# A planned instruction order made anew: a port shared by two engines, a cap on filling matmuls, other stage offsets

## The chip, the cores and the metric

The kernel runs on one core of a Trainium2 chip. The core has a matmul engine (TensorE, PE in the profile; its weight loads are listed apart as PEld), VectorE (DVE), ScalarE (ACT), GpSimd (POOL) and SyncE (SP), which issues transfers. Each engine works through its own queue in order; semaphores hold an instruction until what it needs is there. The metric is device time in microseconds (us), the median of several runs.

## What is computed

Three blocks follow each other, on 4 batches: a recurrence over 768 steps for 32 heads of width 40, a mixing block with a two-dimensional Fourier transform and an MLP, and a second mixing block with two MLPs (w_tok1 768x256, w_tok2 256x768, w_ch1 320x1536, w_ch2 1536x320; those of the first block 320x1280 and 1280x320). The weights arrive in double precision.

```python
for t in range(S):                                  # B=4, H=8, S=768, D=40
    y[:, :, t] = einsum('bhd,bhde->bhe', rt, state)
    Sa = einsum('bhde,bhe->bhd', state, at)
    state = state * wt[:, :, None, :] - einsum('bhd,bhe->bhde', Sa, bt) + einsum('bhd,bhe->bhde', vt, kt)
...
u = x + real(fft(fft(x, axis=1), axis=2))           # x: 4 x 768 x 320
un = (u - mean(u)) / sqrt(var(u) + 1e-06)
x = u + maximum(un @ w_ch1, 0) @ w_ch2
...
h = maximum(x.transpose(0, 2, 1) @ w_tok1, 0) @ w_tok2
u = x + h.transpose(0, 2, 1)
out = u + maximum(u @ w_ch1, 0) @ w_ch2
```

## The kernel before

**First stage, the recurrence (class `Attn`).** It is worked out in 12 chunks of 64 steps, all heads together (33 places in 11 groups of 3). For each chunk: the loads (wS, bt, a, LT, VZt, VZd, r); `decay`, the running products of w as two DVE scans (Q L262, R L265, with a reciprocal L264 between) and their products into a (L269) and bt (L274), on DVE for the first chunks and on POOL afterwards; `kg`, matmuls (L297) whose results are moved into RT (L303 and on ACT) and masked on POOL (L307). Parts of RT go through memory (Gd) into N. For each pair of chunks `inv` forms 32x32 triangular inverses on DVE alone: a copy to start (L333), then pairs of a product into pr (L331) and a sum (L332), copies L337 and L345, and last the copy into MT (L353). The tiles N, Mt, MT and pr exist once. The inverse leaves through memory (Ad, Md) and comes back as AT and Mst for the `merge` matmuls (mg L372, mc L382). `chain` is the step from chunk to chunk: x (L424) from the state LT, its copy bdX (L429), z (L436), s (L448), then on DVE the addition of s to LT in four pieces (L452), on POOL their product (L454), and so the next x. `outp` makes the chunk's result: matmuls st, zt, sc (L486) and y (L504, L508), masks on DVE (L491) and POOL (L496), and evictions into ys (L521, stored) or straight into X (L514) for the last chunks. So an inverse needs kg of its pair, kg needs RT free from an x five chunks earlier, and z of a pair needs its inverse.

**Beside it,** `wdec` (12 jobs) and `decode` (44 jobs) split the weights into a high and a low part: four DVE instructions each (L571 to L575; L780, L781, L783, L784), one on ACT and two on POOL.

**Then the MLPs (class `Mlp`).** `fft`: F, ef and the low part Xl on DVE (L805 to L815), psA matmuls (L824), evictions A on ACT and DVE (L831 to L833), a mirrored copy of A on ACT (L836); `fft2`: mix (L851); normalization, transposes (trp L888), the channel MLP (hps L917, acc L907, with hh on ACT and hl on DVE) and the two of the second block (tps, t2ps). 384 to 447 us is where one stage runs into the other.

**What sets the order.** All instructions are handed to `Plan` as operations with an engine, a cost in us and the tiles that they read and write. `emit` first works out a latest start for each (from a due time of the stage, costs and hand-over times `LATE`, `EXTRA` and `LATE_SAME`), adds an offset of its stage and chunk from the table `OFF`, and then plays the kernel through: at each step it takes the engine that can start first, and there, of the operations that are ready, the one with the earliest latest start. `HOLDBACK` lets an engine wait for one that is due much earlier. The order that comes out is the order in which each engine's queue is written; no time of the plan is kept in the program. Before an operation of TensorE that would have to wait, `fill` puts dummy matmuls `warm` on the identity (L52) into the planned gap: `FILL` holds the planned time of one and a count of columns. If the columns planned over the last `TICK` are under the count, the whole gap is filled.

## Time and profile before

| | |
|---|---|
| median of 3 runs | 1033.73 us (1024.39 to 1034.62) |
| profiled execution: span | 1027.9 us; its own time is not given apart from it |
| TensorE busy | 993.2 us, 97%; of it `warm` 101.5 us, 760 records |
| DVE busy | 635.6 us, 62% |
| ACT, POOL busy | 422.8 and 339.8 us |
| chain that ended last | TensorE 73%, DVE 14%, transfers 6% |
| first z, last y, first hps | 92.7, 406, 446.6 us |

One `warm` matmul is two records of the trace, so 760 records are 380 matmuls. The span is the time from the first to the last instruction of the profiled execution. The chain that ended last is followed back from the last instruction; a line of it says where the end came from, and the busy shares alone do not. The three marks divide the span: up to the first z the first inverse is made, up to the last y the chunks follow each other, and from the first hps on the MLPs run.

### The profile page before, as it was taken

To read this page: it belongs to the slowest core of one execution; us is meant where nothing else is said; L and a number is where in the kernel's file an instruction comes from. 1 tells how busy PE (TensorE), PEld (TensorE's weight loads), DVE (VectorE), ACT (ScalarE), POOL (GpSimd) and SP (SyncE) were. 2 spreads that over 40 slices of the span, in tenths; PEclk is the share of its full clock that TensorE was granted. 3 is DMA by queue.
4 is the path that set the end of the run, shared out by engine and by line. 5 is a ranking of instruction groups with operands and counts; after the bars stand their busy time and mean duration, and the time that the engine had idled before them with its cause. 6 is when DMAs were issued, how large, how long until landed. Compare 5 with 4: busy or idle time off the path is not lost.

```text
span 1027.9 us, 24475 instructions
## 1 busy us (share of the span) xinstructions
PE 993.2 (97%) x10135; PEld 951.4 (93%) x10135; DVE 635.6 (62%) x1346; ACT 422.8 (41%) x870; POOL 339.8 (33%) x425
## 2 busy tenths in 40 slices
PE   8898999899999999899999999999999999999998
PEld 8897888787888988899999999999999999999998
DVE  7598589788978539797888885334432432332322
ACT  4256587686766755342343422223221221221221
POOL 8584377668754544302344434100000000000000
PEclk9999699999999999899999999999999999999999
DMA  9986596989877887822454545900000000000000
GB/s 209 196 169 149 132 210 144 183 183 218 185 177 163 229 236 217 276 66 68 146 158 158 166 142 162 377 1 1 1 20 1 20 1 20 20 1 20 20 21 19
DMA packets 140722, 125.51 MB, mean 122 GB/s; under 512 B 100867, under 2 KB 118275, under 8 KB 140483
## 3 DMA queue, kind: packets, MB, share of 16 engines
q1 hardware_dynamic: 135811, 100.29, 39.6%
q0 software_dynamic: 4800, 23.67, 6.7%
q8 instruction: 79, 1.29, 0.6%
q14 instruction: 32, 0.26, 0.1%
HBM read 85.40 MB, written 33.75 MB: 116 GB/s over the span
## 4 chain that ended last, share of the span: by engine, by line
PE 73%; DVE 14%; DMA 6%; issue 2%; POOL 2%; SPq 2%; ACT 1%; DVEq 0%; POOLq 0%; ACTq 0%
PE hps L917 22%; PE acc L907 21%; DVE pr L331 4%; PE warm L52 4%; PE sc L486 3%; PE mix L851 3%; PE psA L824 2%; PE kg L297 2%; PE t2ps L994 2%; PE tps L981 2%; DMA Mst<-Md 2%; PE y L508 2%; SPq L217 1%; PE trp L888 1%; PE x L424 1%
## 5 line engine op out<-in xcount | busy, mean ns | idle before, releaser
L920 DVE SCALAR_TENSOR_TENSOR hl<-hps,hh 128x384 fp32r<-128x384 f32 x176 | 97.8, 556 | 239.0 <-ACT hh L919 238.4
L919 ACT ACTIVATE hh<-hps 128x384 fp32r<-128x384 f32 x176 | 86.4, 491 | 306.9 <-PE hps L917 306.9
L917 PE MATMUL hps<-th,v 128*128 128x384 f32 x576 | 143.0, 338 | 0.0
L907 PE MATMUL acc<-v,hh 128*128 128x320 f32 x576 | 129.5, 311 | 0.0
L917 PE MATMUL hps<-th,W 128*128 128x384 f32 x480 | 119.7, 339 | 0.9 <-DVE th L893 0.6
L907 PE MATMUL acc<-W,hh 128*128 128x320 f32 x480 | 107.9, 311 | 0.0
L52 PE MATMUL warm<-ident 128*128 128x128 f32 x760 | 101.5, 288 | 5.4 <-DVE A L833 3.4
L917 PEld LDWEIGHTS hps<-th,v 128*128 128x128 f32 x576 | 103.8, 188 | 0.2
L52 PEld LDWEIGHTS warm<-ident 128*128 128x128 f32 x760 | 96.2, 202 | 6.6 <-issue 3.5
L907 PEld LDWEIGHTS acc<-v,hh 128*128 128x128 f32 x576 | 97.6, 188 | 0.0
L785 POOL TENSOR_TENSOR mda<-mda,mdh 128x320 f32<-128x320 f32 (+2 forms) x44 | 44.4, 1009 | 153.9 <-ACT mdh L782 111.0
L917 PEld LDWEIGHTS hps<-th,W 128*128 128x128 f32 x480 | 86.8, 188 | 2.5 <-DVE th L893 1.0
L907 PE MATMUL acc<-v,hl 128*128 128x320 f32 x288 | 89.0, 309 | 0.0
L907 PEld LDWEIGHTS acc<-W,hh 128*128 128x128 f32 x480 | 80.8, 188 | 0.0
L907 PE MATMUL acc<-W,hl 128*128 128x320 f32 x240 | 74.0, 308 | 0.0
L917 PE MATMUL hps<-tl,v 128*128 128x384 f32 x192 | 64.6, 337 | 0.0
L307 POOL TENSOR_SCALAR_AFFINE_SELECT RT<-RT 64x384 f32<-64x384 f32 x72 | 52.6, 756 | 33.7 <-ACT RT L219 32.3
L297 PE MATMUL kg<-am,bt 120*128 120x192 f32 x242 | 52.2, 352 | 8.0 <-issue 2.6
L486 PE MATMUL sc<-rm,VZd 120*128 120x192 f32 x264 | 57.0, 350 | 2.1 <-DMA VZd<-in_vR_dram 1.0
L907 PEld LDWEIGHTS acc<-v,hl 128*128 128x128 f32 x288 | 54.1, 188 | 0.0
L917 PE MATMUL hps<-tl,W 128*128 128x384 f32 x160 | 53.9, 337 | 0.0
L496 POOL TENSOR_SCALAR_AFFINE_SELECT sc<-sc 64x384 f32<-64x384 f32 (+1 forms) x72 | 44.0, 612 | 27.3 <-ACT sc L219 24.7
(175 smaller groups left out, 2090.7 us busy)
## 6 DMA issues: line engine op xcount, KB each, us to landing
bt<-in_bkR_dram SPq DMA_DIRECT2D x12, 660.0 KB
mdraw<-in_moe_w_ch_dram SPq DMA_DIRECT2D x22, 320.0 KB
wS<-in_wR_dram SPq DMA_DIRECT2D x12, 335.2 KB
a<-in_aR_dram SPq DMA_DIRECT2D x12, 335.2 KB
RT<-a SPq DMA_DIRECT2D x36, 111.7 KB
LT<-in_vT_dram SPq DMA_DIRECT2D x12, 330.0 KB
VZt<-in_vT_dram SPq DMA_DIRECT2D x12, 330.0 KB
r<-in_rR_dram SPq DMA_DIRECT2D x12, 330.0 KB
```

The source lines that it names most:

```text
L52: for x in range(m): nc.tensor.matmul(t[:,128*(x%4):128*(x%4)+128],lhsT=ident,rhs=ident,start=True,stop=True)
L297: nc.tensor.matmul(ps[:,192*x:192*x+192],lhsT=bt[:,g+x].rearrange("p v t -> p (v t)"),rhs=am[:,:,g+x],start=True,stop=True)
L307: nc.gpsimd.affine_select(out=kv,in_=kv,pattern=[[0,3*m],[1,L]],compare_op=ALU.is_gt,fill=0.0,base=0,channel_multiplier=-1)
L331: P.op('DVE',.16+.0012*st[0]*shape[0],lambda: V.tensor_tensor(out=pr,in0=a,in1=b,op=ALU.mult),rd,[('pr',h)])
L486: for x,g in enumerate(gs): nc.tensor.matmul(ps[:,192*x:192*x+192],lhsT=VZd[:,g].rearrange("p v t -> p (v t)"),rhs=s.rm[:,:,g],start=True, ...
L496: nc.gpsimd.affine_select(out=o,in_=o,pattern=[[0,3*m],[1,L]],compare_op=ALU.is_gt,fill=0.0,base=0,channel_multiplier=-1)
L785: P.op('POOL',.06+d*.0028,lambda: nc.gpsimd.tensor_tensor(out=g("da").bitcast(F32),in0=g("da").bitcast(F32),in1=g("dh").bitcast(F32),op=AL ...
L851: nc.tensor.matmul(s.pst(h)[:,:320],lhsT=aa[:K,sl],rhs=T2[:K,tb],start=n==0,stop=n==7)
L907: nc.tensor.matmul(s.pst(acc[x]),lhsT=a[:,sl],rhs=t[w2][w][:,m],start=(m==0 and n==0),stop=(m==MT-1 and n==2))
L917: for n,(l,r) in enumerate(ops): nc.tensor.matmul(ps,lhsT=l,rhs=r,start=n==0,stop=n==7)
L919: s.act(384,lambda: nc.scalar.activation(out=t["hh"][z],in_=s.pst(h),func=AF.Relu),[kp],[('hh',z)],free=[h[0]])
L920: s.dve(.47,lambda: nc.vector.scalar_tensor_tensor(out=t["hl"][z],in0=s.pst(h),scalar=0.0,in1=t["hh"][z].bitcast(F32),op0=ALU.max,op1=ALU. ...
```

## The change

The planner gets one more rule, other costs and other offsets, and so a new order of the same instructions.

- An operation has a flag `port`: set for POOL operations without a transfer (not for memsets) and for those DVE operations that read two inputs from the on-chip memory, and some copies. `held` keeps which engine holds the port pair and until when. An operation with the flag starts, in the plan, only when the other engine has let go; among those that are ready the time it would wait counts with the weight `PW` against it.
- The costs are new: hand-over times smaller, scans 1.56 for 1.84, POOL's masks and products cheaper, issuing a transfer .5 for .64 (SP) and for 1.1 (POOL), DVE's decode .24 for .38 and alike. TensorE's costs are as before.
- `fill` puts in at most as many `warm` as bring the count of columns up to `FILL[1]`, which is 8203.8 for 9558.7; that is 17 at most in one gap.
- `HOLDBACK` is 1110 for 394.6, and every number of `OFF` is new.

```diff
-LATE={'ACT':.16,'DVE':.18,'POOL':.1,'PE':.3}
-EXTRA={'ACT':.08,'DVE':.035}
-LATE_SAME={'DVE':.03,'ACT':.03}
+LATE={'ACT':.135,'DVE':.115,'POOL':.09,'PE':.25}
+EXTRA={'ACT':.01}
+LATE_SAME={}
...
+        o.port=(eng=='POOL' and not data) if port is None else port
...
-        dma=0.0
+        dma=0.0; held=[None,0.0]
+        def port(o): return held[1] if o.port and held[0]!=o.eng else 0.0
...
-            m=0; o=Op(); o.eng='PE'; o.idx=-1; o.deps=[]; o.cost=FILL[0]; o.cols=512.0; a=t+.1
-            while b and a+FILL[0]<=end: a=s.pe(a,o); m+=1
+            m=0; top=-int(-(FILL[1]-w)//512); o=Op(); o.eng='PE'; o.idx=-1; o.deps=[]; o.cost=FILL[0]; o.cols=512.0; a=t+.1
+            while b and m<top and a+FILL[0]<=end: a=s.pe(a,o); m+=1
...
-                if pick is None or lst[o.idx]<lst[pick.idx]: pick=o
+                l=lst[o.idx]+PW*max(port(o)-t,0.0)
+                if pick is None or l<best: pick,best=o,l
...
-            engines[e]=s.pe(t,o) if e=='PE' else t+o.cost
+            b=max(t,port(o))
+            engines[e]=s.pe(b,o) if e=='PE' else b+o.cost
+            if o.port: held=[e,engines[e]]
...
-HOLDBACK=394.60
+PW=54.4
+HOLDBACK=1110.0
...
-OFF={'chain': -53.3, 'dec2': -42.2, 'decay': -47.7, 'decode': -65.8, 'fft': 52.7, 'fft2': -1.1, 'inv': 6.1,
+OFF={'chain': -50.3, 'dec2': 73.3, 'decay': -47.8, 'decode': -137.2, 'fft': 137.1, 'fft2': -148.5, 'inv': 6.5,
...
-FILL=(0.22,9558.7)
+FILL=(0.22,8203.8)
```

Each engine has the same instructions after as before, save for `warm`: 254 matmuls for 380, of which 114 for 226 stand ahead of the first z, 103 for 79 from there to the last z, 3 for 25 from there to the first psA, and 24 for 40 from there to the first hps. Lines are 4 to 5 higher in the changed kernel (L331 is L335, L805 is L810).

The first place is DVE's queue in the middle and at the end of the first inverse. Q, R and wS are the operands of the scans, D those of the reciprocal, pr, MT and Mt the inverse's. Before, the middle:

```order
L331 TENSOR_TENSOR pr_121<-Mt_119,MT_120 128x512 x2
L332 TENSOR_REDUCE Mt_119<-pr_121 128x8x8 x2
L262 SCALAR_TENSOR_TENSOR Q_112<-wS_111,D_113 120x715
L345 COPY MT_120<-Mt_119 128x256
L264 RECIPROCAL D_114<-Q_112 120x11
L331 TENSOR_TENSOR pr_121<-N_118,MT_120 128x256
L331 TENSOR_TENSOR pr_121<-N_118,MT_120 128x512
L332 TENSOR_REDUCE MT_120<-pr_121 128x16x4
L265 SCALAR_TENSOR_TENSOR R_126<-wS_111,D_114 120x715
L332 TENSOR_REDUCE MT_120<-pr_121 128x16x4
```

After, its end and the start of the second inverse (the last row):

```order
L336 TENSOR_REDUCE Mt_119<-pr_121 128x2x16
L269 SCALAR_TENSOR_TENSOR R_130<-wS_110,D_114 120x715
L336 TENSOR_REDUCE Mt_119<-pr_121 128x2x16
L357 COPY MT_120<-Mt_119 128x1024
L266 SCALAR_TENSOR_TENSOR Q_112<-wS_111,D_113 120x715
L268 RECIPROCAL D_114<-Q_112 120x11
L269 SCALAR_TENSOR_TENSOR R_126<-wS_111,D_114 120x715
L337 COPY Mt_119<-N_118 128x4
```

The scans Q and R of chunk 5 (R_126) stood in the middle and stand behind the copy of MT; R of chunk 4 (R_130) has moved from the inverse's start to its end, and a third scan Q that stood further on in it is gone from it.

The second place is DVE's queue in the third inverse, with the additions to the state (LT_136). Before, where they begin:

```order
L331 TENSOR_TENSOR pr_121<-Mt_119,MT_120 128x512 x2
L332 TENSOR_REDUCE Mt_119<-pr_121 128x8x8 x2
L452 TENSOR_TENSOR LT_136<-s,LT_135 40x320
L345 COPY MT_120<-Mt_119 128x256
L452 TENSOR_TENSOR LT_136<-s,LT_135 40x320
L331 TENSOR_TENSOR pr_121<-N_118,MT_120 128x256
L331 TENSOR_TENSOR pr_121<-N_118,MT_120 128x512
L332 TENSOR_REDUCE MT_120<-pr_121 128x16x4
L452 TENSOR_TENSOR LT_136<-s,LT_135 40x320
L265 SCALAR_TENSOR_TENSOR R_128<-wS_111,D_114 120x715
L332 TENSOR_REDUCE MT_120<-pr_121 128x16x4
```

After, where the same inverse ends:

```order
L335 TENSOR_TENSOR pr_121<-Mt_119,MT_120 128x448
L336 TENSOR_REDUCE Mt_119<-pr_121 128x2x16 x2
L357 COPY MT_120<-Mt_119 128x1024
L456 TENSOR_TENSOR LT_136<-s,LT_135 40x320 x4
L266 SCALAR_TENSOR_TENSOR Q_112<-wS_110,D_113 120x715
L268 RECIPROCAL D_114<-Q_112 120x11
L433 COPY bdX_142<-x 64x8x40
```

The four additions stood between the pairs of the inverse and stand behind its last copy, ahead of bdX.

The third place is TensorE's queue ahead of the first mix (psA and Xh are of `fft`, A of its evictions). Before:

```order
L824 MATMUL psA_5621<-T_4838,Xh 128x192 x2
L824 MATMUL psA_5621<-T_4838,Xl 128x192
L824 MATMUL psA_5637<-T_4838,Xh 128x192 x2
L824 MATMUL psA_5637<-T_4838,Xl 128x192
L52 MATMUL warm<-ident 128x128 x23
L851 MATMUL mix<-T_5481,A_5482 128x320 x2
L851 MATMUL mix<-T_5481,A_5483 128x320
```

After:

```order
L829 MATMUL psA_5430<-T_4739,Xl 128x192
L829 MATMUL psA_5441<-T_4739,Xh 128x192 x2
L829 MATMUL psA_5441<-T_4739,Xl 128x192
L52 MATMUL warm<-ident 128x128 x17
L856 MATMUL mix<-T_5452,A_5453 128x320 x2
L856 MATMUL mix<-T_5452,A_5454 128x320
```

Both have a filling there, of 23 matmuls before and of 17 now.

The last is DVE's queue at the evictions A that this filling and mix wait for; mdt and mda belong to the decoding of weights. Before:

```order
L806 TENSOR_TENSOR ef_4847<-F 128x3x159
L833 TENSOR_TENSOR A_5486<-psA_5545,A_5486 64x193
L781 SCALAR_TENSOR_TENSOR mda_5489<-mdraw_5487,mdt_5488 128x320
L832 TENSOR_TENSOR A_5485<-psA_5621,A_5484 128x193
L783 TENSOR_SCALAR mdt_5488<-mda_5489 128x320
L832 TENSOR_TENSOR A_5483<-psA_5637,A_5482 128x193
L780 TENSOR_SCALAR mdt_4850<-mdraw_4849 128x320
L784 SCALAR_TENSOR_TENSOR mdt_5488<-mdraw_5487,mdt_5488 128x320
L833 TENSOR_TENSOR A_5486<-psA_5545,A_5486 64x192
L832 TENSOR_TENSOR A_5485<-psA_5621,A_5484 128x192
L832 TENSOR_TENSOR A_5483<-psA_5637,A_5482 128x192
```

After:

```order
L810 TENSOR_TENSOR F<-X 128x960
L811 TENSOR_TENSOR ef_4934<-F 128x3x159
L838 TENSOR_TENSOR A_5457<-psA_5406,A_5457 64x193
L837 TENSOR_TENSOR A_5456<-psA_5430,A_5455 128x193
L837 TENSOR_TENSOR A_5454<-psA_5441,A_5453 128x193
L817 TENSOR_TENSOR Xl<-ef_4933,Xh 128x3x33
L838 TENSOR_TENSOR A_5457<-psA_5406,A_5457 64x192
L837 TENSOR_TENSOR A_5456<-psA_5430,A_5455 128x192
L837 TENSOR_TENSOR A_5454<-psA_5441,A_5453 128x192
```

The decode instructions stood between the evictions of A and are gone from there; from the first F up to the evictions one decode job of four instructions is left of about six.

## Rows read from the trace of the kernel before

**Rows 1.** The page, part 2: TensorE's granted clock in 40 slices of the span.

```profile
PEclk9999699999999999899999999999999999999999
```

**Rows 2.** Windows, all engines: stretch, length, busy us (count), PEclk, DMA share, GB/s.

```profile
0.00:93.00 93.00, 84.26 (x853) 82.13 (x854) 70.17 (x106) 44.66 (x70) 65.41 (x82) 0.98 0.86 183
...
120.00:384.00 264.00, 250.96 (x4732) 220.57 (x4732) 202.81 (x381) 186.72 (x357) 166.55 (x216) 0.99 0.83 190
...
447.00:1028.00 581.00, 575.95 (x3714) 572.58 (x3712) 287.49 (x673) 150.57 (x337) 76.50 (x86) 1.00 0.21 68
```

**Rows 3.** Windows for the tile warm alone, same columns, TensorE only.

```profile
0.00:93.00 93.00, 56.57 (x452) 55.24 (x452) 0.98 0.86 183
93.00:384.00 291.00, 23.61 (x158) 20.74 (x158) 0.96 0.81 186
384.00:447.00 63.00, 18.47 (x130) 17.45 (x130) 0.92 0.75 232
447.00:1028.00 581.00, 2.87 (x20) 2.76 (x20) 1.00 0.21 68
```

**Rows 4.** Timeline of DVE, start: start us, us, instruction, [idle before, released by].

```profile
21.41 0.88 DVE L278 TENSOR_SCALAR rm<-a,hm 120x704 f32<-120x704 f32 x1
...
25.94 1.65 DVE L262 TENSOR_TENSOR_SCAN Q<-wS,D 120x715 f32<-120x715 f32 x1 [1.04 <-POOL R L268]
...
40.27 1.65 DVE L262 TENSOR_TENSOR_SCAN Q<-wS,D 120x715 f32<-120x715 f32 x1 [10.36 <-DMA wS<-in_wR_dram]
```

**Rows 5.** Timeline of DVE, first inverse and start of the second.

```profile
41.83 0.14 DVE L333 COPY Mt<-N 128x4 f32<-128x4 f32 x1
...
46.42 1.94 DVE L331 TENSOR_TENSOR pr<-Mt,N 128x196 f32<-128x196 f32 x1
...
56.34 1.80 DVE L262 TENSOR_TENSOR_SCAN Q<-wS,D 120x715 f32<-120x715 f32 x1
...
60.57 2.30 DVE L265 TENSOR_TENSOR_SCAN R<-wS,D 120x715 f32<-120x715 f32 x1
...
68.27 1.93 DVE L262 TENSOR_TENSOR_SCAN Q<-wS,D 120x715 f32<-120x715 f32 x1
...
77.01 1.30 DVE L353 COPY MT<-Mt 128x1024 f32<-128x1024 f32 x1
...
83.44 0.57 DVE L333 COPY Mt<-N 128x4 f32<-128x4 f32 x1 [3.48 <-DMA Ad<-MT]
```

**Rows 6.** Timeline of POOL beside it.

```profile
46.30 1.70 POOL L269 TENSOR_TENSOR a<-a,R 120x715 f32<-120x715 f32 x1 [9.90 <-DMA a<-in_aR_dram]
```

**Rows 7.** Windows of line L331 (pr) over the inverses: length, busy (count).

```profile
41.80:78.40 36.60, 16.90 (x22) 0.95 0.87 180
83.40:117.60 34.20, 12.20 (x22) 0.78 0.58 126
...
sum 237.40, DVE 84.99; mean DVE 14.17
```

**Rows 8.** Timeline, third inverse: last LT addition and bdX on DVE; TensorE's x.

```profile
158.59 0.49 DVE L452 TENSOR_TENSOR LT<-s,LT 40x320 f32<-40x320 f32 x1
...
171.76 0.90 DVE L429 COPY bdX<-x 64x320 f32<-64x320 f32 x2
...
164.31 1.13 PE L424 MATMUL x<-LT,RT 128*64 128x40 f32 x32
```

**Rows 9.** Chain that ended last, 380 to 430 us: start us, us, what.

```profile
395.32 0.32 DVE mdt L780
...
418.99 0.40 DVE mdt L784
```

**Rows 10.** Timelines of ACT and TensorE before the first mix.

```profile
419.81 1.35 ACT L836 ACTIVATE A<-A 128x384 fp32r<-128x384 f32 x3 [0.52 <-DVE A L833]
...
419.93 7.00 PE L52 MATMUL warm<-ident 128*128 128x128 f32 x46 [3.39 <-DVE A L833]
```

**Rows 11.** Windows around the stretch at the lower clock, columns as in rows 2.

```profile
102.80:120.00 17.20, 17.20 (x192) 14.56 (x194) 12.09 (x25) 6.31 (x12) 4.63 (x8) 0.50 0.53 144
```

More of the change, by code (lines that the diff above doesn't have):

```diff
@@ L54 @@
 class Op:
-    __slots__=('eng','cost','fn','deps','succ','due','alloc','free','data','idx','fin','nwait','ready','rel','cols','stage','pools')
-LATE={'ACT':.16,'DVE':.18,'POOL':.1,'PE':.3}
-EXTRA={'ACT':.08,'DVE':.035}
-LATE_SAME={'DVE':.03,'ACT':.03}
+    __slots__=('eng','cost','fn','deps','succ','due','alloc','free','data','idx','fin','nwait','ready','rel','cols','stage','pools','port')
+LATE={'ACT':.135,'DVE':.115,'POOL':.09,'PE':.25}
+EXTRA={'ACT':.01}
+LATE_SAME={}
 class Plan:
@@ L64, in __init__, with op @@
         s.ops=[]; s.w={}; s.r={}; s.banks=banks; s.stage=None; s.filler=None
-    def op(s,eng,cost,fn,R=(),W=(),due=None,alloc=None,free=(),data=0.0,rel=0.0,after=(),cols=0.0,pools=None):
-        o=Op(); o.cols=cols; o.stage=s.stage; o.pools=pools; o.rel=rel; o.eng,o.cost,o.fn,o.due,o.data=eng,cost+EXTRA.get(eng,0.0),fn,due,data
+    def op(s,eng,cost,fn,R=(),W=(),due=None,alloc=None,free=(),data=0.0,rel=0.0,after=(),cols=0.0,pools=None,port=None):
+        o=Op(); o.cols=cols; o.stage=s.stage; o.pools=pools; o.port=(eng=='POOL' and not data) if port is None else port; o.rel=rel; o.eng,o.cost,o.fn,o.due,o.data=eng,cost+EXTRA.get(eng,0.0),fn,due,data
         o.alloc=[] if alloc is None else alloc if isinstance(alloc,list) else [alloc]
@@ L220, in zero @@
     def zero(s,t,W,cost=.3):
-        s.P.op('POOL',cost,lambda: s.nc.gpsimd.memset(t,0.0),(),W)
+        s.P.op('POOL',cost,lambda: s.nc.gpsimd.memset(t,0.0),(),W,port=False)
     def one(s,t,W,v=1.0):
-        s.P.op('POOL',.1,lambda: s.nc.gpsimd.memset(t,v),(),W)
+        s.P.op('POOL',.1,lambda: s.nc.gpsimd.memset(t,v),(),W,port=False)
     def init(s):
@@ L344, in inv @@
         d0=16*33; K=((0,4),(4,4),(8,2),(10,2),(12,2),(14,2))
[L345 removed]
+        P.op('DVE',.29,lambda: V.tensor_copy(out=tt(512,[16,16],[1,16]),in_=mm(d0,[1,16],[32,16])),['m8',('m16',1)],['mt2'],port=True)
         for t0,w in K:
@@ L352, in inv @@
         mk=['m8','Mt']+[('m16',m) for m in range(2)]+[('m32',x) for x,_ in K]
-        P.op('DVE',1.08,lambda: V.tensor_copy(out=s.MT,in_=s.Mt.rearrange("p i j -> p j i")),mk,['MT','mt1','mt2']+[('t2',x) for x,_ in K])
+        P.op('DVE',.97,lambda: V.tensor_copy(out=s.MT,in_=s.Mt.rearrange("p i j -> p j i")),mk,['MT','mt1','mt2']+[('t2',x) for x,_ in K],port=True)
         for x in range(2):
@@ L544, in out_tile @@
         P.op('NONE',0.0,close,[],keys+['close'])
-        for k in range(3): P.op('POOL',1.0,lambda k=k: nc.gpsimd.dma_start(out=s.T1[:,k],in_=s.T1d[128*k:128*k+128]),['close'],[('T1',k)],data=2.2)
+        for k in range(3): P.op('POOL',.5,lambda k=k: nc.gpsimd.dma_start(out=s.T1[:,k],in_=s.T1d[128*k:128*k+128]),['close'],[('T1',k)],data=2.2)
         for x in range(f):
@@ L693, in pe, with dve @@
         s.P.op('PE',cost,fn,R,W,alloc=alloc,due=s.now,cols=cols); s.now+=cost
-    def dve(s,cost,fn,R,W,free=()): s.P.op('DVE',cost,fn,R,W,free=free)
+    def dve(s,cost,fn,R,W,free=(),port=False): s.P.op('DVE',cost,fn,R,W,free=free,port=port)
     def act(s,n,fn,R,W,free=()): s.P.op('ACT',.05+n/1200,fn,R,W,free=free)
@@ L807, in fft @@
-                s.dve(.07+.167*w,lambda ef=ef,K=K: nc.vector.tensor_tensor(out=ef()[:,K,161:320],in0=t["F"][:,K,1:160],in1=t["F"][:,K,319:160:-1],op=ALU.subtract),kk('F'),kk(*kE,1))
-                s.dve(.07,lambda ef=ef,K=K: nc.vector.tensor_copy(out=ef()[:,K,0:161:160],in_=t["F"][:,K,0:161:160]),kk('F'),kk(*kE,0))
+                s.dve(.06+.336*w,lambda par=par,k0=k0,k1=k1,K=K: nc.vector.tensor_tensor(out=t["F"][:,K],in0=x()[:,K],in1=x()[:,3+k0:3+k1],op=ALU.add if par==0 else ALU.subtract),xk+['mid0']+([('x',i,b) for i in range(6)] if not s.first[b] else []),kk('F'),port=True)
```

122 lines of the change are left out of this document (61 added, 61 removed), and 6 rows, old and new, of the table OFF.

## Prediction

> **What bounds the kernel now.** I read the page first. TensorE is busy for 97% of the span (the table above), and its granted clock is full or nearly so in all but one of the 40 slices [rows 1]. That looks like a kernel bound by TensorE throughout, and it is not: part of the busy time is `warm`, dummy matmuls on the identity that only fill gaps. So the second view is a table of stretches, the third the same table for `warm` alone. From 447 us on, in the MLPs, TensorE is busy for 575.95 of 581 us and only 2.87 us of that are `warm` [rows 2, 3]. That stretch has nothing to give. Before it, `warm` takes 56.57 us up to 93 us, 23.61 up to 384 and 18.47 up to 447: 98.65 us in which TensorE waits for someone, filled so that it looks busy. From 0 to 93 us DVE (70.17) and POOL (65.41) work hard and TensorE's own work is 84.26 - 56.57 = 27.69 us. From 120 to 384 TensorE's work is some 227 to 251 of 264 us and DVE's 202.81, so there neither is alone the limit: the loop of state, inverse and transfer is.
>
> Third, DVE's timeline at the start shows the path to the first inverse: `rm` is made at 21.41 behind the scan Q of chunk 2, the last RT eviction of chunk 1 behind the scan Q of chunk 3 (25.94), then the transfers, and DVE idles 10.36 us until the scan at 40.27 can run [rows 4]. Then the first inverse runs from 41.83 to 78.3, in order, and the second starts at 83.44 when Ad, made of the first, has landed [rows 5]. In the first inverse stand three foreign scans. Last, the end of the first stage (384 to 447) by the chain of waits: DVE's decode instructions and `warm` stand in it [rows 9, 10].
>
> The sum is made on the profiled span, 1027.9; the time of that execution is not given apart from it. The median of the runs is 1033.73, 5.8 above it, and I carry the sum over to the median.
>
> **The change, part by part.** Every engine issues the same instructions; only the order and the number of `warm` change.
>
> *Start.* `rm` and the RT evictions of chunk 1 move ahead of scans: the scan (1.65) and the wait of DVE ahead of it (1.04) go from in front of the last eviction. TensorE's kg matmuls must also come earlier, which they can, since they waited for `rm`, now behind one scan less. A load (LT) moves ahead of a load that the path needs, which costs a fraction of a microsecond. I take **-2.0**; bounds 0 (kg does not come earlier) and -2.7 (1.65 + 1.04).
>
> *First inverse.* Three scans of 1.80, 2.30 and 1.93 leave it: 6.03 us [rows 5]. In the order after, two of them stand behind the copy of MT. From the end of that copy (77.01 + 1.30) to the landing of Ad at 83.44 DVE had 5.1 us, 3.48 of it idle and the rest weight decoding, so two scans (1.80 + 2.30 = 4.1) are covered by the transfer of Ad; if that cover is gone, they cost 4.1 again. The third comes in a later gap. What was decoded there moves further back, where DVE has slack. I take **-6.0**; bounds -1.9 and -6.0.
>
> *Middle, 93 to 384.* In inverses 1 to 5 some foreign DVE work is moved out too, and the state's additions LT of chunks 1, 3, 7 and 9 move from inside the inverse to its end or behind it. Before, the additions of chunk 3 ran until 159.08; the next thing of the chain on DVE, bdX, stood behind the copy of MT that ends the inverse anyway, at 171.76 [rows 8]. Four additions of 0.49 (2.0), a product on POOL and x (1.13) now go between: about 4 us each time with the product put at the length of x, against an inverse that is shorter by its additions (2.0) and by other moved work. I call the sum of both **-2** with bounds -8 (2 won at each of four) and +8 (2 lost at each).
>
> *Port pair.* The planner now keeps DVE instructions with two inputs from running beside POOL's. The row for which this speaks: `pr` of 128x196 took 1.94 us while POOL's product `a` of 1.70 ran from 46.30 on [rows 5, 6], and `pr` alone costs 12.20 us in one inverse and up to 16.90 in another [rows 7]. All six against the cheapest: 84.99 - 6 x 12.20 = 11.8 us. But nothing in the program holds an engine: it only stands in another order, and the queues run free. I count nothing, with -11.8 as the bound; waiting for the port could also cost, but that is in the +8 above. The Trainium skill ("SBUF — State Buffer", section "Who interferes with whom") says that the port pair shared by DVE and GpSimd is an exclusive lock, that a DVE instruction with two SBUF inputs meets a GpSimd one that reads SBUF, and that the order of issue decides who is blocked. The row agrees with it; by that rule alone an order without meetings would give back the whole excess and the sum would be 11.8 us lower.
>
> *End of the first stage.* On the chain from 380 to 430 us stand eleven pieces of weight decoding on DVE, 4.5 us in all; the first and the last of them are shown, and the last four stand among the evictions A [rows 9]. In the order after one decode job of four instructions remains there, the others stand behind A. I take 3.5 of the 4.5. Then `warm`: 23 matmuls (46 records) from 419.93 take 7.00 us, until 426.93, and mix is behind them, though ACT had ended the mirror that mix reads at 421.16 [rows 10]. So the filling itself is up to 5.8 us of delay. In the order after it is 17: 17 x 7.00/23 = 5.2, so 1.8 less. Together **-5.3**; bounds -1.8 (decode hidden by other waits) and -10.3 (4.5 + 5.8). What is decoded later has to be ready for the MLP; there DVE is busy 287 of 581 us [rows 2], which hides it.
>
> *MLPs:* 0, since TensorE is dense and its own instructions are the same.
>
> Sum: -2.0 - 6.0 - 2.0 - 5.3 = -15.3; on the median 1033.7 - 15.3 = 1018.4, so **1018**.
>
> **The rivals.**
> *Nothing comes out (chance 0.18).* The earlier state is given back in later waits, as TensorE has its 227 us of work from 120 to 384 and the loads come when they come; only the 1.8 of the count and the start's 2.0 stay: 1030. For it: TensorE is busy nearly everywhere. Against it: 42 us of `warm` behind 93 us and 13 us of idle time are slack in the stretch.
>
> *The port pays (chance 0.10).* If the new order really keeps the products of DVE and POOL apart, all six inverses cost pr what the cheapest costs now: 1018.4 - 11.8 = 1007. For it: the 1.94 beside POOL's 1.70. Against it: one late engine shifts the queues against each other, and the plan's separation is gone. The rule for it is that of the Trainium skill's page on SBUF, named above.
>
> *The clock (chance 0.12).* Less `warm` (254 matmuls for 380) leaves TensorE less busy in the gaps. The row for its price: from 102.8 to 120 us the granted clock was 0.50, the lower of its two levels (1.2 for 2.4 GHz), with 192 records in 17.20 us, right after a stretch of many small matmuls and waits [rows 11]; at full clock the same would take half, so 8.6 us are lost in such a stretch when it lies on the path. Three more of these: 1018 + 25.8 = 1043.8; two: 1035. Against it: that stretch came with the full filling too, so it isn't the filling alone that holds the clock, and the early gaps, where most `warm` goes, have little on TensorE's path. The Trainium skill ("TensorE: Matmul & The Clock Gate", Part 1) says that the throttled state is the default and activity releases it, which speaks against a smaller filling; the row agrees in that the clock does fall inside the kernel.
>
> *The state behind the inverse (slower, chance 0.12).* If x of chunks 1, 3, 7 and 9 waits for the end of the inverse on DVE, then kg, its transfers and the next inverse wait too. Price: 4 us each (above), and waits for the port may lengthen the inverse by as much as the 16.90 differs from 12.20, 4.7 more, so up to 8.7. Four times 8.7 is 34.8; less the other terms (2.0 + 6.0 + 5.3 = 13.3) that makes 1033.7 + 21.5 = 1055. It decides from 5.9 us a time: four of them are 23.6, the 13.3 and the 10.3 that a measurement can tell. Against it: bdX stood behind the same copy before.
>
> **How the numbers follow.** The forecast has 0.48, with a range of its own of 1010 to 1023: the sum with the bounds of start and end of stage. With the port's 0.10, which is also faster by over 1%, that is 0.58. A measurement of this kernel can tell about 1%, 10.3 us, from no change; so under 1023.4 is faster and above 1044 slower. Faster 0.58. Same: 0.18 of the first rival, 0.07 of the clock (two stretches) and 0.03 of the third, 0.28. Slower: 0.05 of the clock (more than three) and 0.09, 0.14. The range goes to 1003, the sum with the port's gain (1006) and 3 of the tail's, and to 1040, where the first rival and two stretches of the lower clock lie; above it about 0.15, below it 0.03.
>
> **What would show it.** The first inverse in the changed kernel: the time from its first copy (L337) to its copy of MT (L357), 35.2 us before (41.83 to 77.01), should be 29 to 30, with one scan in it instead of four; it should start at 39 to 40. z of chunk 0, at 92.7 before (the table above), at 84 to 85. The third inverse (138 to 172 before) should end near 163, and x of chunk 3 start behind its end within 4 us. The `warm` ahead of the first mix: 5.2 us rather than 7.0, the first hps 15 us earlier (446.6 before), and from there to the end 581 us as now. `pr` per inverse: if it falls to 12 each, the port was worth it, and I am too high. It would be wrong if the granted clock stands at 0.5 for tens of microseconds between 93 and 384, or if DVE in the inverses waits for PE's s at the LT additions, or if hps starts at 440 or later.

## The result and the profile after

The changed kernel takes **1040.65 us** (1035.78 to 1047.44) against 1032.42 (1024.39 to 1036.77) for the kernel before in the same comparison: ratio 1.0116, interval 1.0088 to 1.0143. It is slower by 1.2% where 1018 was forecast. Ratios, and the mean granted clocks given further down, are over the fast executions alone, those within 1.5% of the fastest of their kernel. The profiled spans are 1037.8 and 1027.9, so 9.9 us are to be explained in them.

Four marks divide that span: first z 92.2 us (92.7 before), first z of chunk 11 393.6 (383.9), first hps 451.3 (446.6), end 1037.8 (1027.9). By stretches that is -0.5, +10.2, -5.0 and +5.2. The loss has two places: the middle, and the MLPs, which were forecast at 0.

Page of the profile after, granted clock in 40 slices (as [rows 1]), then windows of all engines (columns as in [rows 2]):

```profile
PEclk9788999998899989999999999999999999999999
```

```profile
0.00:93.00 93.00, 67.29 (x649) 62.68 (x651) 69.32 (x102) 45.26 (x70) 57.23 (x80) 0.85 0.88 182
120.00:384.00 264.00, 242.20 (x4368) 214.01 (x4367) 197.51 (x359) 167.65 (x320) 148.21 (x198) 0.94 0.75 171
...
447.00:1038.00 591.00, 583.36 (x3755) 579.08 (x3753) 301.68 (x701) 156.29 (x352) 88.86 (x100) 1.00 0.24 77
```

From 120 to 384 every engine is busy less than in [rows 2]: TensorE 242.20 for 250.96, DVE 197.51 for 202.81, POOL 148.21 for 166.55, transfers .75 for .83. No engine has become the bound; all wait more. The same for `warm` alone (as [rows 3]):

```profile
0.00:93.00 93.00, 31.22 (x228) 29.83 (x228) 0.85 0.88 182
93.00:384.00 291.00, 29.71 (x206) 25.89 (x206) 0.94 0.74 170
384.00:447.00 63.00, 8.97 (x54) 8.10 (x54) 0.96 0.68 212
```

DVE's timeline at the start and in the first inverse (as [rows 4, 5]):

```profile
27.96 0.42 DVE L307 TENSOR_SCALAR RT<-kg,sg 128x192 f32<-128x192 f32 x1 [2.28 <-PE kg L301]
...
41.51 1.65 DVE L266 TENSOR_TENSOR_SCAN Q<-wS,D 120x715 f32<-120x715 f32 x1 [7.64 <-DMA wS<-in_wR_dram]
43.08 0.15 DVE L337 COPY Mt<-N 128x4 f32<-128x4 f32 x1
...
72.19 1.03 DVE L357 COPY MT<-Mt 128x1024 f32<-128x1024 f32 x1
73.14 1.64 DVE L266 TENSOR_TENSOR_SCAN Q<-wS,D 120x715 f32<-120x715 f32 x1
...
81.38 0.17 DVE L337 COPY Mt<-N 128x4 f32<-128x4 f32 x1 [3.61 <-DMA Md<-Mt]
```

The inverse starts 1.25 us later than before and its last copy begins 4.8 us earlier, at 72.19 for 77.01. The second inverse gains only 2.1 of that (81.38 for 83.44). The rest went on SP, the queue that hands out the transfers. The first inverse leaves by Md and Ad, and ahead of these SP holds N of chunk 3, which waits until that chunk's Gd has landed, three loads of RT and one of wS. Two transfers from the chain of waits, then SP's timeline:

```profile
68.22 3.69 DMA Gd<-RT
...
76.41 5.34 DMA Ad<-MT
```

```profile
71.97 0.52 SPq L221 DMA_DIRECT2D N<-Gd  x1
72.58 2.72 SPq L221 DMA_DIRECT2D RT<-a  x3
...
75.96 0.39 SPq L221 DMA_DIRECT2D Md<-Mt  x1
76.41 1.79 SPq L221 DMA_DIRECT2D Ad<-MT  x2
```

The copy had ended at 73.22; Ad left SP 3.2 us later and took 5.34 us. Md left 0.45 us ahead of Ad, and it is Md that the second inverse waited for last. The waits of the whole span, before and after (engine, line and what it waited for: us in total, times, longest):

```profile
POOL bt L274 <- DMA bt<-in_bkR_dram: 4.2, 4, 1.6
```

```profile
POOL bt L278 <- DMA bt<-in_bkR_dram: 25.2, 5, 13.3
...
PE x L428 <- DMA RT<-a: 7.2, 3, 6.0
```

The loads of bt come late in the middle: 21.7 to 28.0 us of such waits stand in the traces of after, r1, r4 and h4 (kernels of the next section), 4.2 and 6.4 in those of before and h3. From the end of the fourth inverse (230.4) to that of the fifth (299.0) the rows show what else stands there:

```profile
232.63 3.80 POOL L278 TENSOR_TENSOR bt<-bt,Q 120x512 f32<-120x512 f32 x3 [13.31 <-DMA bt<-in_bkR_dram]
235.33 2.92 PE L301 MATMUL kg<-am,bt 120*128 120x192 f32 x8
255.25 0.27 DVE L337 COPY Mt<-N 128x4 f32<-128x4 f32 x1 [1.20 <-DMA Mst<-Md]
281.52 1.65 DVE L269 TENSOR_TENSOR_SCAN R<-wS,D 120x715 f32<-120x715 f32 x1 [6.04 <-PE pt L398]
297.98 1.06 DVE L357 COPY MT<-Mt 128x1024 f32<-128x1024 f32 x1
```

Marks of the kernels that the next section speaks of, read from their DVE and TensorE timelines in us (an inverse from its first copy to the end of its last, numbered from 1):

| kernel | inverse 1 | inverse 2 starts | inverse 4 | inverse 5 | inverse 6 | z of chunk 11 | first hps | span |
|---|---|---|---|---|---|---|---|---|
| before | 41.8-78.3 | 83.4 | 183.2-232.9 | 247.3-285.4 | 299.6-344.5 | 384 | 446.6 | 1027.9 |
| after | 43.1-73.2 | 81.4 | 195.8-230.4 | 255.3-299.0 | 310.6-352.1 | 394 | 451.3 | 1037.8 |
| h1 | 42.4-71.7 | 82.3 | 180.2-233.0 | 246.3-289.9 | 303.1-354.4 | 394 | 459.0 | 1039.1 |
| h3 | 42.2-78.1 | 83.3 | 183.8-232.3 | 245.6-287.2 | 300.5-348.6 | 386 | 446.0 | 1032.6 |
| h4 | 42.5-72.4 | 81.4 | 202.6-236.4 | 260.4-305.9 | 317.5-357.3 | 396 | 480.0 | 1060.2 |
| r3 | 43.6-74.1 | 81.8 | 199.7-234.1 | 251.0-293.2 | 304.6-351.1 | 401 | 457.7 | 1046.0 |
| s2 | 43.8-73.3 | 81.5 | 210.6-244.4 | 268.3-308.0 | 334.6-377.0 | 416 | 480.4 | 1063.7 |
| q2 | 43.4-72.8 | 80.9 | 197.7-232.7 | 253.9-290.1 | 311.5-347.3 | 394 | 449.9 | 1038.6 |
| q6 | 47.7-77.3 | 89.6 | 217.5-261.6 | 284.2-323.3 | 342.1-381.6 | 439 | 494.8 | 1081.9 |

Each row is one execution, and executions differ. Up to z of chunk 11 h4 has the order of the kernel after, and r1 has it throughout but for the number of `warm`; their fourth inverses start at 202.6 and 201.4 where that of the kernel after starts at 195.8. So a single mark can differ by 7 us with no change of order. What holds in all of these traces is the loss of the middle: z of chunk 11 comes at 394 to 396 in after, r1 and h4, at 384 and 386 in before and h3.

In the kernel after, the fourth inverse ends 2.5 us earlier than before; the fifth ends 13.6 later. Between the two ends lie 68.6 us for 52.5 (64.7 to 69.5 in after, r1 and h4, 52.5 and 54.9 in before and h3), which is more than the whole loss of the middle.

### The profile page after: what moved, and what is told of

Same layout as the page of the kernel before. It is cut to its first block, busy times and chain, and to the rows that moved or that the text cites. A ratio compares the mean times of both kernels' runs of the same rounds, so it can differ in the third digit from the quotient of the medians.

```text
span 1037.8 us, 24005 instructions
## 1 busy us (share of the span) xinstructions
PE 976.4 (94%) x9883; PEld 931.1 (90%) x9883; DVE 642.6 (62%) x1346; ACT 420.9 (41%) x870; POOL 329.3 (32%) x425
## 4 chain that ended last, share of the span: by engine, by line
PE 66%; DVE 16%; DMA 7%; ACT 5%; issue 3%; SPq 1%; POOL 1%; DVEq 0%; ACTq 0%; POOLq 0%
PE hps L922 21%; PE acc L912 20%; PE kg L301 4%; PE sc L490 3%; PE warm L52 3%; PE t2ps L999 2%; PE tps L986 2%; DVE pr L335 2%; SPq L221 1%; PE y L512 1%; PE trp L893 1%; DMA AT<-Ad 1%; DMA m11l<-mda 1%; PE psA L829 1%; PE y L508 1%
## 5 line engine op out<-in xcount | busy, mean ns | idle before, releaser
L790 POOL TENSOR_TENSOR mda<-mda,mdh 128x320 f32<-128x320 f32 (+2 forms) x44 | 45.5, 1035 | 136.5 <-ACT mdh L787 103.0
L52 PE MATMUL warm<-ident 128*128 128x128 f32 x508 | 72.6, 293 | 8.8 <-DVE A L837 3.6
L52 PEld LDWEIGHTS warm<-ident 128*128 128x128 f32 x508 | 66.4, 204 | 10.2 <-issue 6.7
L301 PE MATMUL kg<-am,bt 120*128 120x192 f32 x242 | 59.1, 392 | 15.4 <-POOL bt L278 8.0
L301 PEld LDWEIGHTS kg<-am,bt 120*128 120x128 f32 x242 | 48.2, 229 | 19.9 <-POOL bt L278 8.1
L500 POOL TENSOR_SCALAR_AFFINE_SELECT sc<-sc 64x384 f32<-64x384 f32 (+1 forms) x72 | 40.2, 559 | 39.2 <-ACT sc L223 36.7
```

The costliest lines, as they stand in the source:

```text
L52: for x in range(m): nc.tensor.matmul(t[:,128*(x%4):128*(x%4)+128],lhsT=ident,rhs=ident,start=True,stop=True)
L301: nc.tensor.matmul(ps[:,192*x:192*x+192],lhsT=bt[:,g+x].rearrange("p v t -> p (v t)"),rhs=am[:,:,g+x],start=True,stop=True)
L500: nc.gpsimd.affine_select(out=o,in_=o,pattern=[[0,3*m],[1,L]],compare_op=ALU.is_gt,fill=0.0,base=0,channel_multiplier=-1)
L790: P.op('POOL',.07+d*.00237,lambda: nc.gpsimd.tensor_tensor(out=g("da").bitcast(F32),in0=g("da").bitcast(F32),in1=g("dh").bitcast(F32),op=A ...
```

## The experiments

Ratios are against the kernel before, measured beside each run, with their 95% intervals. Most edits work on the planner's result: it plans once, which gives the kernel's own order, and plans again by the place that each operation had, with some places edited. Without an edit the order comes out as it was, but for the joined lists, which are said below. `warm` is still put in by the planner's rule where nothing else is said, so an edit changes the number of these matmuls too. The cuts of code are shortened: names stand for lists of operation numbers.

**The fill counts, exchanged.** Order of the one kernel, number of `warm` in each gap by the rule of the other.

```diff
-            if b and not first: s.seq.append(('F',b,m))
+            if b and not first: s.seq.append(('F',b,other))
```

> The changed kernel with every operation on every engine in its own order; only the number of warm matmuls in each gap is that of the old rule (329 for 254). In the changed kernel the granted clock is at its lower level for some 75 us before the MLPs (before: about 41 us), and TensorE's own instructions take 903.8 us for 891.7. Theory A (the cap on filling costs the time): the lower level shrinks to 40 to 50 us, the first kg after the start comes faster, and the time is 8 to 12 us below the changed kernel, at the level of the kernel before. Theory B (the order costs the time, by the state's chain): within 3 us of the changed kernel, since what TensorE does slowly is waited for by nobody.

> The kernel before with every operation in its own order; only the number of warm matmuls in each gap is that of the new rule (276 for 380). Theory A (the cap costs the time): 6 to 12 us slower than before, with 30 us more at the lower clock. Theory B (the order costs it): within 3 us of before; the shorter filling ahead of the first mix (17 for 23) gives back 1.8 us of it.

Measured: r1, the new order with 329 `warm`, 1.0126 (1.0088 to 1.0163); r2, the old order with 276 for 380, 0.9972 (0.9938 to 1.0007). So a quarter fewer `warm` cost nothing in the old order, and 30% more won nothing in the new one: the cap isn't the cause.

The lower clock itself isn't settled by this. In the profiled executions it stood for 37.5 us ahead of the MLPs before, 68.3 after and 54.6 in r1. Of the 30.7 us more after, 23.9 lie ahead of 93 us, where the first z comes no later, and 10.2 from 93 to 384. At a granted 0.50 [rows 11] TensorE does half its work, so of the 10.2 us that the middle lost, at most some 5 (an estimate) are lost by the clock directly. Over many executions of one kernel, though, clock and time go together: of 69 of the kernel before, measured beside the runs, the third with the highest mean granted clock (0.988) took 1024.8 us on average, the third with the lowest (0.977) 1032.7, and each of the five comparisons by itself leans the same way. A straight line through the 69, carried on to the 0.964 of the kernel after, gives 1041, all that was lost. Against it: r2 has 0.973 and lies 8 us below that line, r1 with 0.969 lies 5 above it. Whether the clock costs time there, or waits cost time and lower the clock, no run separates.

**Single stalls taken out of the new order.** r3 puts the state's additions, products and x of chunk 3 back into the third inverse; r4 puts Md and Ad of the first inverse on SP ahead of the N, RT and wS that stood before them; s1 does r3 and moves the end of decay 7 and kg 7 up as well.

```diff
+def MOD(p,ops):
+    for at,g in MOVES:
+        for n,x in enumerate(g): p[x]=at+n/100
+MOVES=[(740,STATE_OF_CHUNK_3)]
```

> The changed kernel, but the four LT additions of chunk 3, their products on POOL, x and bdX of chunk 3 are moved up in the list that sets the order, to where s of chunk 2 is done; the rest is listed as in the changed kernel. Theory B (the state waits behind the inverse): x of chunk 3 at 155 to 160 us instead of 172, the fourth inverse starts at 184 to 188 instead of 196, and the time is 5 to 10 us below the changed kernel. Theory A (clock): the gain is given back behind it, within 2 us of the changed kernel.

> The changed kernel, but on SP the transfers Md and Ad of the first inverse go ahead of five that stood before them (N and RT of chunk 3 and a load). Theory: of the 6 us that left the first inverse 3 were lost in SP's queue, where Ad stood behind transfers that wait; the second inverse starts at about 78.5 instead of 81.4 and z of chunk 0 comes at 89 instead of 92; if the start carries through, the time is 3 us below the changed kernel. Rival: the start is not what the later chunks wait for, and the time is the same within 1 us.

> The changed kernel, but in the list that sets the order three groups of chunk 3 and chunk 7 go up together: the LT additions, products and x of chunk 3 (as in the run on LT alone, where x of chunk 3 came 14 us earlier and the fourth inverse did not), the end of decay of chunk 7 (R on DVE, a on POOL), and kg of chunk 7 with its evictions and transfers. Theory: two things met at the fourth inverse, and each alone hid the other; now kg of chunk 7 comes at 163 to 170 instead of 179, the fourth inverse starts at 182 to 187 instead of 196, and the time falls by 5 to 9 us against the changed kernel. Rival: the loop closes at the next joint again (LT additions of chunk 4 behind the third inverse, merge); then the fourth inverse starts early, but the time stays within 2 us.

Measured: r3 1.012 (1.0076 to 1.0164), r4 1.0131 (1.0094 to 1.0168), s1 1.0131 (1.009 to 1.0172); the change itself 1.0116. r3 and r4 did what they were for. TensorE's timeline for the first half of x of chunk 3, after and in r3:

```profile
171.88 1.36 PE L428 MATMUL x<-LT,RT 128*64 128x40 f32 x32 [0.89 <-POOL LT L458]
```

```profile
157.75 1.14 PE L443 MATMUL x<-LT,RT 128*64 128x40 f32 x32
```

x is 14 us earlier, and the fourth inverse starts at 199.7, no earlier than in the traces of the order without the edit (195.8 to 202.6). In s1 it starts at 192.1, somewhat earlier, and takes 47.5 us for 34.6. In r4 the second inverse starts at 78.8, 2.6 earlier, and ends at 118.7, 5.6 later (in r1, without this edit, at 117.2). No gain is left at the end; as far as single traces tell, each is lost at the next place where stages wait for each other.

**Parts of the two orders joined.** The list of operations of one kernel up to a z, then that of the other for what is left: h1 has the new order to z of chunk 0, h2 the new one from there to z of chunk 11, h3 the new one from z of chunk 11, h4 the new one up to it. What one list had issued before the cut and the other had not is made up right behind it, and the banks of TensorE's results are given out in turn. What a joint and this way of writing cost by themselves was not measured.

```diff
+LIST=joined((before,Z11),(after,END))
```

> Orders of both kernels put together: up to the last z of chunk 0 every engine follows the changed kernel, behind it the order of before (operations that before had already issued by then are made up right after the cut). The first two inverses are then those of the changed kernel. If its start is worth what was forecast (-8.0), the kernel is 6 to 9 us faster than before. Rival: in the changed kernel z of chunk 0 comes only 0.7 us earlier, since the transfer Ad leaves SP late; then the time is that of before within 2 us.

> Up to the last z of chunk 0 the order of before, from there to the last z of chunk 11 that of the changed kernel, then that of before again. If the middle (state behind the inverse, kg late) is what made the change slow, this kernel is 8 to 12 us slower than before, and z of chunk 11 comes at about 394 instead of 384. Rival: the loss belongs to the start or the end; then it is within 3 us of before.

> The order of before up to the last z of chunk 11, then that of the changed kernel. Forecast for this part: -5.3 and nothing in the MLPs. In the changed kernel the way from z of chunk 11 to the first hps is 5.3 us shorter (57.3 for 62.6), but from hps to the end it is 5.2 us longer (586.5 for 581.3). If the shorter way is a gain, the time is 5 us below before; if work only went from ahead of hps to behind it, the time is that of before within 2 us.

> The order of the changed kernel up to the last z of chunk 11, behind it that of before. If the three parts add up, this is the changed kernel less its end: 10 us slower than before when the loss lies in start and middle, and the sum of the two runs on start and middle alone. A difference of more than 4 us from that sum says that the parts don't add, and that an order fits only what goes before it.

Measured: h1 1.0106 (1.0074 to 1.0138), h2 1.0333 (1.0292 to 1.0373), h3 1.0053 (1.0024 to 1.0082), h4 1.0363 (1.0323 to 1.0403). The parts don't add: 1.06, 3.33 and 0.53% against 1.16 for the whole; some of the excess can be the joints' own. h4 has the new start and middle and reaches z of chunk 11 at 396, as the kernel after does, but its first hps at 480 for 451: the old end, joined so, doesn't fit behind the new middle. h1 makes its first inverse as short as forecast (29.3 us) and is no faster for it: z of chunk 11 comes at 394.

h3 settles the last stretch. Windows from the first hps to the end, all engines, of before, after and then, for `mix` alone, before and h3:

```profile
446.60:1027.90 581.30, 576.35 (x3716) 572.98 (x3715) 287.89 (x674) 150.97 (x338) 76.50 (x86) 1.00 0.21 68
```

```profile
451.30:1037.80 586.50, 579.06 (x3725) 574.78 (x3723) 298.06 (x693) 154.66 (x348) 87.03 (x97) 1.00 0.23 77
```

```profile
446.60:1027.90 581.30, 21.09 (x137) 20.26 (x136) 8.70 (x18) 1.00 0.21 68
```

```profile
446.00:1032.60 586.60, 22.88 (x144) 21.46 (x144) 8.58 (x18) 1.00 0.24 77
```

The new end has 5.2 us more behind the first hps: 2.7 of TensorE's work, of it 1.8 `mix` that stood ahead of hps before, and 2.5 of idle time. h3 has the old start and middle and the same 586.6. Its way from z of chunk 11 to the first hps is 3.1 us shorter (59.6 for 62.7), the rest of its span 5.3 longer. So the new end by itself is no gain: the shorter way to the first hps was in part work moved behind it.

**Rules in place of the table.** The state's chain is listed ahead of everything that is ready in s2 (new list) and s4 (old list), and in s3 the chain, then kg, then merge (new list).

```diff
+def MOD(p,ops):
+    for o in ops:
+        if o.stage and o.stage[0] in ('chain',): p[o.idx]-=1e6
```

> The list of the changed kernel, but of what is ready the state's chain (x, bdX, z, s, LT) goes first on every engine, for all chunks. Theory (the state waits behind inverses at chunks 1, 3 and 7): the LT additions stand inside the inverses, x of chunk 3 at about 157 and x of chunk 7 at about 275, z of chunk 11 at 384 to 388, time 6 to 10 us below the changed kernel. Rival: what the chain takes on DVE makes the inverses longer by as much, and the time is within 3 us of the changed kernel or above it.

> As the run with the chain first, and behind the chain kg with its transfers and then merge, ahead of everything else (weight decoding, chunk results, transposes, decay). Theory (it is the loop of chain, kg and merge that sets the pace): z of chunk 11 at or before 384, time at or below the kernel before (1028 to 1033). Rival: decay and the transposes feed that loop and now come late; slower than the changed kernel by 5 us or more.

> The list of the kernel before with the same rule, the chain first. There the LT additions already stand inside the inverses. Theory: little to win, within 4 us of before. If it is slower by 5 us or more, an order is so closely fitted to its own table that moving any stage in it costs, and the same holds for the changed kernel.

Measured: s2 1.0364 (1.0322 to 1.0405), s3 1.0451 (1.041 to 1.0493), s4 1.0395 (1.0349 to 1.0441). x of chunk 3 runs at 153 in s2, 19 us earlier, and the fourth inverse starts at 210.6 instead of 195.8. With r3 this speaks against the theory that the middle waits for the state alone. It isn't a clean test: r3 and s2 have 206 and 215 `warm` for 254, and 109 and 106 us at the lower clock for 68.3.

**Late loads.** q1 moves the loads of bt for chunks 9 to 11 and the transposes that free their buffers up; q2 also moves the second scan of chunk 11 out of the fifth inverse. Their expectations count the inverses from 0, so the fourth there is the fifth here.

```diff
+MOVES=[(1011,KBT_5),(1036.5,[BT_9]),(1145,KBT_6),(1150.5,[BT_10]),
+       (1255,KBT_7),(1290,[BT_11]),(1545.5,[R_SCAN_11])]
```

> The changed kernel's list with the loads of bt for chunks 9 to 11, and the kbt transposes that free their buffers, moved up (on SP the load of chunk 9 stands 11 places earlier). Theory that the late loads make the loss between the third and the fourth inverse: the products' waits for bt fall from 25.2 us to under 10, kg of chunk 9 starts before 231 (235 now), the fourth inverse ends at 294 or earlier (299 now), and the whole comes to about 1035 (ratio 1.005). Rival, that an order fits only what stands ahead of it: the waits fall but z of chunk 11 stays within 3 us of 394 and the ratio within 1.009 to 1.016. A third outcome, the waits do not fall: then the load is late for another reason than its place, and this theory isn't tested.

> As the run before, and the second scan of chunk 11 moved behind the fourth inverse's transposing copy, so that its wait of 6.04 us for a buffer stands no longer inside that inverse. Theory of late loads and a stall inside the inverse: the fourth inverse takes 38 to 40 us (43.7 now), ratio 1.000 to 1.005. Rival (given back at the next joint): the fourth inverse is shorter, the fifth starts later after it or lasts longer, ratio 1.009 to 1.016.

Measured: q1 1.0161 (1.0092 to 1.023); its waits for bt stayed at 26.4 us in all though the load of chunk 9 was issued at 207 for 223, so it tests little. q2 1.0144 (1.0108 to 1.018). There the waits fell by half, and the fifth inverse took 36.2 us for 43.7. Waits, and DVE's timeline of the fifth inverse and of the start of the sixth:

```profile
POOL bt L293 <- DMA bt<-in_bkR_dram: 12.2, 4, 5.7
```

```profile
253.92 0.61 DVE L352 COPY Mt<-N 128x4 f32<-128x4 f32 x1 [2.62 <-DMA N<-Gd]
289.01 1.05 DVE L372 COPY MT<-Mt 128x1024 f32<-128x1024 f32 x1
311.47 0.17 DVE L352 COPY Mt<-N 128x4 f32<-128x4 f32 x1 [1.43 <-DMA N<-Gd]
```

It ends at 290.1 for 299.0, and the sixth starts at 311.5 for 310.6. Nine microseconds won, all of them waited for again. Late bt and the scan in the inverse do lengthen the fifth inverse; with half of these waits and the scan gone the kernel is as slow as with them.

**The table without the refit, and orders close by.** q3 has all new rules and costs with the old offsets and hold-back. q4 moves every place in the old list by a random number of up to 12, q5 by up to 3, q6 the new list by up to 3 with q5's numbers. The planner's rule then fills the gaps anew: 459 `warm` in q4 and 367 in q5 for 380, 156 in q6 for 254.

```diff
+def MOD(p,ops):
+    import random; g=random.Random(1)
+    for o in ops: p[o.idx]+=g.uniform(-3,3)
```

> The changed kernel's planner (port rule, cap on filling, new costs) with the offsets and the hold-back of before. If the new rules and costs lose by themselves, whatever the table: 1.010 to 1.016, as the whole change. If the table loses and the rules gain what they were counted to: 0.990 to 1.000. If rules and table only fit together: above 1.02, worse than either kernel.

> The list of before with every operation's place moved by a random number of up to 12 places either way (some 1,600 operations), the rest as it is; no rule is changed. If the order of before is fitted so closely that any neighbour loses: 1.010 or more, and the changed kernel's loss needs no single cause. If an order is good or bad by its large features: 0.995 to 1.005, and the loss has a cause that can be named.

> As the run with places moved by up to 12, in the list of before, by up to 3 places. If the order is fitted down to single places: 1.01 to 1.03. If only shifts of the size of a stage's step matter, as a cause that can be named would need: 0.997 to 1.005.

> The same by up to 3 places in the changed kernel's list, with the same random numbers. If both lists are fits of the same kind, the changed one only less good: it loses about as much against the changed kernel as the other against before, 1.02 to 1.04 against before. If the changed kernel's list is a loose one, not fitted at this grain: 1.008 to 1.016.

Measured: q3 1.0458 (1.0378 to 1.0538), q4 1.047 (1.0399 to 1.054), q5 1.0051 (1.0002 to 1.01), q6 1.0521 (1.0442 to 1.0601). The old list stands shifts of three places nearly unharmed; the new one is slower by 1.0521/1.0116, 4.0%, with them. Page and window of q6:

```profile
PEclk9788869897889796899999999999999999999999
```

```profile
93.00:400.00 307.00, 273.81 (x4656) 237.64 (x4651) 217.80 (x408) 186.81 (x351) 152.90 (x202) 0.84 0.69 156
```

and the same window after:

```profile
93.00:400.00 307.00, 284.01 (x5108) 249.97 (x5104) 230.58 (x423) 196.61 (x381) 167.38 (x223) 0.94 0.75 174
```

q6 does less of everything in the same stretch, as the change did against before, only more so; it spends 153.6 us at the lower clock for 68.3. These are one draw of numbers each, so how brittle a list is on average is not known, and in q6 the 98 fewer `warm` and the lower clock may have a part in it. What they show is that shifts of a few places, with no rule changed, can cost anything from 0.5% (q5) to 4% (q6 against the kernel after), and shifts of up to 12 places 4.7% (q4); the change lost 1.2%. So a loss of that size needs no single cause. That this one has none is not shown. In q5 POOL waits 16.2 us for bt against 4.2, at a cost of 0.5%, so such waits alone cost little there too. q3 loses as much as q4: with the old table the new rules make an order that is no better than one shifted at random, and the refitted table wins most of that back, though not all. Whether the rules are bad by themselves can't be told from that, since an order that nobody fitted loses that much anyway.

## Why the prediction was wrong, step by step

- **What bounds the kernel.** Right that the middle is a loop of state, inverse and transfers and that neither TensorE nor DVE is its limit alone. Wrong in what was made of it: as if a microsecond taken from a link came out at the end. r3, r4 and q2 took 2.6 to 14 us from a link each, s1 moved two links up at once, and none moved the end forward.
- **Start, -2.0.** Failed. TensorE's kg came no earlier, DVE waited 2.28 us for it, and the last eviction of chunk 1 ran at 27.96 (27.77 before). The scan ahead of the inverse waited for wS until 41.51 (40.27 before): +1.25. wS left SP 1.1 us later, behind N, which waited for the first Gd; and that Gd went out 2.6 us later (23.99 for 21.43), since an eviction of RT ahead of it now stands behind the scan R on DVE as well as behind Q. From the chain of waits after, then wS on SP after and before:

```profile
24.37 6.70 DMA Gd<-RT
```

```profile
35.90 0.55 SPq L221 DMA_DIRECT2D wS<-in_wR_dram  x1
```

```profile
34.78 0.58 SPq L217 DMA_DIRECT2D wS<-in_wR_dram  x1
```

  The load of LT that was costed at a fraction is not on this path; the order on SP behind Gd is, and it had no term.
- **First inverse, -6.0.** Its length was right: 36.5 us became 30.1, with one scan in it. The step that failed is the cover: the two scans behind the copy were hidden by Md and Ad, but these were late on SP behind N, RT and wS; of the 5.1 us by which the inverse ended earlier 2.1 were left where the second starts, and 0.5 at the first z. That transfer queue was not counted. h1, with an inverse of 29.3 us, is no faster either.
- **Middle, -2, bounds -8 and +8.** It was +10.2, outside. The bounds came from one mechanism, additions to the state at four places, and x of chunk 3 did come later, its first half by 16 us (171.88 for 156.2), its second by 14 (178.3 for 164.31 [rows 8]). But undoing it in r3 brings nothing. What stands in the trace of the kernel after is 25.2 us of waits for bt (4.2 before), a wait of 6.04 for a scan's buffer inside the fifth inverse, and more idle time on every engine. None of it was in the sum, since the rows of before had next to none: a new order makes its own waits. That these are the cause is not shown; q2 took a good part of them out and is no faster.
- **Port pair, 0.** Right, and for the reason given: the queues run free, and products of the two engines still run beside each other (rows at the end). Windows of pr per inverse (as [rows 7]):

```profile
43.00:73.30 30.30, 15.74 (x22) 0.83 0.81 164
...
sum 215.20, DVE 87.99; mean DVE 14.67
```

  pr takes 87.99 us for 84.99, no less, with the rule in the planner. The rival of 1007 is out.
- **End of the first stage, -5.3.** Right in size up to the mark (62.7 to 57.7 us, -5.0): the filling ahead of mix starts 31.6 us behind z of chunk 11 for 36.0, and takes 5.61 us as against 5.2 forecast and 7.00 before.

```profile
425.24 5.61 PE L52 MATMUL warm<-ident 128*128 128x128 f32 x34 [3.57 <-DVE A L837]
```

- **MLPs, 0.** Failed by +5.2, and this cancels the step before it. The work that was taken from the chain ahead of hps stands behind it, where TensorE was said to be dense. h3 shows this by itself, 1.0053.
- **The rivals.** The nearest in mechanism is the first, that a gain is given back in later waits; its 1030 took for granted that nothing is lost. The clock did fall for longer, by 30.7 us, close to two of the stretches for which the clock's rival said 1035; r1 and r2 show that the cap on `warm` isn't what cost the time, and how much of it the lower clock carries stays open. The state behind the inverse occurred, and taking it out of chunk 3 brought nothing. By the prediction's own limits (1023.4 and 1044) the result is "same", for which it gave 0.28; the interval shows that it is a small loss. The range ended at 1040; the median is 1040.65. Its inner range began at 1010, said to be the sum with the bounds of start and end; those bounds make it 1012.7.
- **Its signs of being wrong.** Two came: the first hps at 451.3, behind 440, and 34 us at the lower clock between 93 and 384 (24 before).

What stays open: which wait makes the middle 10 us longer. Each one that was removed was followed by another, and no version faster than before by more than its interval was found (r2, 0.9972, is the best). Open too is the lower clock's part. The step of the prediction that failed is known all the same: it added terms, each read from one link, as if they came out at the end. The start gave +1.25 for -2.0, the first inverse passed on 0.5 of its 6.0, the middle gave +10.2 for -2, and the 5.0 won ahead of the first hps were lost behind it.

## What to carry to other kernels

A written order of thousands of instructions can be fitted to its own waits, as both lists were here: a link of a loop that gets shorter counts for nothing until the links behind it are shown to have been waiting for that one, and forecasting a re-fitted order by the sum of its improved rows leaves out the waits that it makes anew. When a stretch gets shorter, look for its instructions behind the mark before counting the gain. And move a list at random by a few places before looking for the cause of one per cent: that tells how large a difference an order can make without a new rule. Draw more than once: one draw here lost 0.5%, another 4%.

## What the runs showed of the hardware that was not expected

104 fewer filling matmuls (276 for 380) in an unchanged order made no measurable difference (0.9972), although the mean granted clock of its executions was 0.973 against 0.982. DVE's products and POOL's met again in spite of the planner's rule: two pr of 128x512 took 2.79 us while POOL's product of 1.78 ran beside them. Before, the same two took 1.29, though a product of POOL (1.69 from 49.74) began while they ran (the last two rows). So in these rows a meeting doesn't always lengthen DVE's side.

```profile
46.14 0.50 DVE L335 TENSOR_TENSOR pr<-Mt,N 128x196 f32<-128x196 f32 x1
47.37 2.79 DVE L335 TENSOR_TENSOR pr<-N,MT 128x512 f32<-128x512 f32 x2
47.83 1.78 POOL L273 TENSOR_TENSOR a<-a,R 120x715 f32<-120x715 f32 x1 [9.86 <-DMA a<-in_aR_dram]
```

```profile
49.09 1.29 DVE L331 TENSOR_TENSOR pr<-N,MT 128x512 f32<-128x512 f32 x2
49.74 1.69 POOL L274 TENSOR_TENSOR bt<-bt,Q 120x512 f32<-120x512 f32 x1 [1.31 <-DMA bt<-in_bkR_dram]
```

The pr of 128x196, which took 1.94 us beside POOL before [rows 5, 6], takes 0.50 in the new place, and the meeting has only moved to the next product.
